# Issuing the first weight load ahead of the opening barrier in a cached-attention decode kernel

## Chip, cores and metric

One core of one Trainium2 chip. The metric is the device time of one execution in microseconds. A ratio between two kernels is the mean time of one kernel's fast runs over that of the other's in the same rounds, so it is not quite the ratio of the medians that are quoted beside it. Some of the traces' records are of single packets of the 16 DMA engines; where a number comes from those and not from a printed view, the text says so. These records name no engine: packets are put down to one engine because each of them starts within some 0.01 us of another's end.

## The reference

A decode step of two sequences with one token each: layernorm, attention with 32 heads over a cache of 8192 positions, an output projection, and a gated feed-forward block. The caches are what matters: 2 x 2 x 32 x 8192 x 128 bf16 values, 268 MB, each read once.

```python
def _A_ref(x, k_cache, v_cache, wq, wo):            # x: (2, 1, 512)
    q = (x @ wq).reshape(B, Sq, Hq, Dh)...           # wq: 512 x 4096
    scores = jnp.einsum("bhqd,bhkd->bhqk", q, k) * (Dh ** -0.5)
    p = _softmax(scores, axis=-1)
    o = jnp.einsum("bhqk,bhkd->bhqd", p, v)
    return o... @ wo                                 # wo: 4096 x 512
h = x + _A_ref(_layernorm(x), A_k_cache, A_v_cache, A_wq, A_wo)
h2 = h + _B_ref(_layernorm(h), B_W_gate, B_W_up, B_W_down)
```

## The kernel before

SyncE does all the large loads. Two SBUF buffers, K and V, each hold one tile of 8.39 MB (128 rows of 64 KB). wq is put into the upper half of V before V's first own tile, so the first V load has to wait for the projection that reads wq. Each engine's program begins with a drain and a barrier that the framework emits (four small constants on POOL, then all five engines meet); what the kernel writes comes behind it.

```python
nc.scalar.dma_start(x_row, A_x[:, 0]).then_inc(sem_x, 16)
nc.sync.dma_start(V[:, SLOT:], A_wq.rearrange("(p c) n -> p (c n)", c=DC)).then_inc(sem_wq, 16)
nc.sync.dma_start(
    wo_rows, A_wo[128 * DR:].rearrange("(p r) n -> p (r n)", r=4)).then_inc(sem_wl, 16)
load(K, A_k_cache, 0, k_sem[0])
# ... constants on POOL, layernorm of x on VectorE (cut) ...
pe.wait((sem_wq, 16), t_xlT, t_zero)      # projection: 32 matmuls over wq
# ... (cut)
sp.wait(t_q)
load(V, A_v_cache, 0, v_sem)              # V's first tile overwrites wq
# ... in each of the 15 later turns (cut):
sp.wait((d2s, 2 * o - 1), tokp("kf", p))  # K free again
load(K, A_k_cache, o, k_sem[0])
sp.wait(tokp("pv", p))                    # V free again
load(V, A_v_cache, o, v_sem)
```

The softmax here doesn't subtract the row's maximum and nothing guards it: scores larger than these inputs give would overflow.

Of the kernel before, what the change touches and what calls it, by code (L numbers as in the profile page):

```python
# [39 lines left out]
def bass_sequential_preLN__gqa_block_cached__glu_gated_reglu__decode_kernel(  # L40
# [16 lines left out]
    DC = D // 128  # L57
# [5 lines left out]
    SLOT = J * Dh  # L63
# [16 lines left out]
    with ExitStack() as es:  # L80
        def S(name):
            return es.enter_context(nc.semaphore(name))

        def sb(name, shape, dt):
            return es.enter_context(nc.sbuf_tensor(name, shape, dt))
# [14 lines left out]
        sem_x, sem_wq, sem_wl, sem_out = S("x"), S("wq"), S("wl"), S("out")  # L100
# [6 lines left out]
        V = sb("V", [128, 2 * SLOT], BF16)  # L107
# [62 lines left out]
        def kv_rows(cache, o):  # L170
            hq, b = divmod(o, B)
            return cache[b, A * hq:A * hq + A].rearrange("h (p j) d -> (h p) (j d)", p=128 // A)
# [4 lines left out]
        if True:  # L177

            def program():

                def load(x, cache, o, sem, k0=0, k1=2 * J):
                    nc.sync.dma_start(
                        x[:, k0 * Dh:k1 * Dh], kv_rows(cache, o)[:, k0 * Dh:k1 * Dh]).then_inc(sem, 16)

                nc.scalar.dma_start(x_row, A_x[:, 0]).then_inc(sem_x, 16)
                nc.sync.dma_start(V[:, SLOT:], A_wq.rearrange("(p c) n -> p (c n)", c=DC)).then_inc(sem_wq, 16)
                nc.sync.dma_start(
                    wo_rows, A_wo[128 * DR:].rearrange("(p r) n -> p (r n)", r=4)).then_inc(sem_wl, 16)
                load(K, A_k_cache, 0, k_sem[0])
# [57 lines left out]
                for k, row in enumerate((x_row, lnx_row)):  # L247
                    rv = row.rearrange("b (n c) -> b c n", c=DC)
                    for c in range(DC):
                        i = nc.tensor.transpose(  # L250
                            Tp[0][:].bitcast(BF16)[:, (k * DC + c) * B:(k * DC + c + 1) * B], rv[:, c, :], ident[0:B, 0:B])
# [9 lines left out]
                for i in range(2):  # L261
                    for c in range(DC):
                        for t in range(4):
                            n = (2 * t + i) * 512
# [20 lines left out]
                for r in range(2):  # L285
                    for h in range(2):
                        i = nc.tensor.matmul(
                            Sp[r][64 * h:64 * h + 64, 0:A * NQ], lhsT=ident[:].rearrange("p (n r) -> p r n", r=2)[:, r, :],
                            rhs=qT[:], start=True, stop=True)
# [184 lines left out]
                for r in range(DR):  # L474
                    i = nc.tensor.matmul(
                        Op[1][32 * (r % 4):32 * (r % 4) + B, :], lhsT=O_all[:, r, :], rhs=X[:, r * D:(r + 1) * D],
                        start=(r < 4), stop=(r >= DR - 4))
# [249 lines left out]
                for h in range(A):  # L727
                    for c in range(DC):
                        i = nc.tensor.matmul(
                            Wp[:, c * B:(c + 1) * B], lhsT=wv[:, h, c, :], rhs=O_keep[:, h, :],  # L730
                            start=False, stop=True, skip_group_check=True)
# [7 lines left out]
                for c in range(DC):  # L739
                    i = nc.tensor.matmul(Sp[0][:, 0:B], lhsT=onesn[:], rhs=hb[:, c * B:(c + 1) * B],  # L740
                                         start=(c == 0), stop=(c == DC - 1))
# [47 lines left out]
                for k in range(2):  # L789
                    i = nc.tensor.matmul(Sp[0][:, 32:32 + B], lhsT=onesn[:], rhs=vh[:, k * B:(k + 1) * B],  # L790
                                         start=(k == 0), stop=(k == 1))
# [20 lines left out]
                for n, (f, k) in enumerate(order):  # L812
                    pe.wait((sem_wd[k], 16))
                    kp = 128 if f < 10 else FR
                    for m in range(4):
                        i = nc.tensor.matmul(  # L816
                            Op[0][32 * m:32 * m + B, 0:128], lhsT=hd[0:kp, f * B:(f + 1) * B],
                            rhs=(wdn[:, f, :] if f < 10 else wd_last[:])[:, 128 * m:128 * m + 128],
                            start=False, stop=(n == FC - 1), skip_group_check=True)
# [12 lines left out]
                nc.sync.wait_ge(sem_out, 16 * B)  # L832

            program()

    return nc
# [28 lines left out]
```

## Time and profile before

| | before |
|---|---|
| time, median of the first 3 runs | 657.58 us (657.36 to 657.63) |
| span of the profiled execution | 656.1 us |
| read from HBM | 281.05 MB, 428 GB/s over the span |
| busiest engine (VectorE) | 66% |
| SyncE's queue, share of the 16 DMA engines | 99.3% |

The lines themselves stand in the prediction. In the chain and timeline views the first number is a start in us from the beginning of the span and the second a duration; for a DMA piece of the chain these are its issue and the time to its landing.

### The profile page before, as it was taken

What the parts mean: (1) busy time and instruction counts of PE and PEld (TensorE: products, weight loads), DVE (VectorE), ACT (ScalarE), POOL (GpSimd) and SP (SyncE); (2) the same over time, 40 slices, a digit from 0 to 9 for tenths busy, and PEclk for the clock granted to TensorE, in tenths of its full rate; (3) what the DMA queues carried; (4) which work ended last, traced back from release to release, by engine and by line L of the source; (5) the groups of instructions that cost most, each with busy time, mean ns of one, the idle gap of its engine ahead of it and who ended that gap; (6) DMA issues with size and microseconds to landing.
All of it is one profiled execution on the core that took longest, in us unless ns stands there. A gap on an engine that the chain in (4) does not pass through costs nothing.

```text
span 656.1 us, 8543 instructions
## 1 busy us (share of the span) xinstructions
PE 371.9 (57%) x3480; PEld 236.3 (36%) x3481; DVE 432.7 (66%) x275; ACT 304.6 (46%) x719; POOL 88.7 (14%) x96
## 2 busy tenths in 40 slices
PE   2374573756457385545637555474755537464677
PEld 0152441615134161423416242251623325152445
DVE  1187493947849395793939669393875939488771
ACT  1355362735536173443716445371653527254460
POOL 4000020030301103030120303003030300303000
PEclk9856556566655756665575667557565655766657
DMA  9999999999999999999999999999999999999997
GB/s 408 401 439 440 447 435 404 443 443 443 416 428 439 447 439 400 443 443 447 420 420 439 447 435 404 447 439 447 428 412 443 443 435 420 431 439 415 430 423 313
DMA packets 6324, 281.16 MB, mean 429 GB/s; under 512 B 710, under 2 KB 812, under 8 KB 1324
## 3 DMA queue, kind: packets, MB, share of 16 engines
q1 hardware_dynamic: 6308, 281.05, 99.3%
q8 instruction: 5, 0.08, 0.1%
q14 instruction: 3, 0.02, 0.0%
q10 hardware_dynamic: 8, 0.00, 0.0%
HBM read 281.05 MB, written 0.00 MB: 428 GB/s over the span
## 4 chain that ended last, share of the span: by engine, by line
DMA 64%; PE 22%; ACT 7%; DVE 6%; issue 1%; DVEq 0%; SPq 0%
DMA K<-in_A_k_cache_dram 59%; PE T L395 16%; ACT kT L578 7%; DMA K<-in_B_W_gate_dram 5%; PE S L378 5%; DVE prod L552 2%; DVE prod L561 2%; DVE X L561 1%; DVE X L552 1%; DVE scores L566 0%; PE O L816 0%; PE O L764 0%; DVEq L617 0%; DVEq L598 0%; DVE kT L824 0%
## 5 line engine op out<-in xcount | busy, mean ns | idle before, releaser
L578 ACT ACTIVATE kT<-T 128x1024 bf16<-128x1024 bf16 x160 | 160.0, 1022 | 196.5 <-PE T L395 192.7
L395 PE MATMUL T<-ident_f,K 128*128 128x128 f32 x640 | 161.7, 416 | 100.7 <-DVEq L598 94.8
L552 DVE TENSOR_TENSOR X<-K,q_c 128x11264 bf16<-128x11264 bf16 x15 | 90.4, 6026 | 172.5 <-DMA K<-in_A_k_cache_dram 172.5
L418 PE MATMUL O<-V,e 128*16 128x512 bf16 x1024 | 117.2, 596 | 111.1 <-ACT e L506 77.0
L395 PEld LDWEIGHTS T<-ident_f,K 128*128 128x128 f32 x640 | 114.5, 213 | 102.8 <-DVEq L598 96.8
L561 DVE TENSOR_TENSOR prod<-prod 128x5632 bf16<-128x5632 bf16 (+1 forms) x68 | 104.3, 1533 | 4.0
L552 DVE TENSOR_TENSOR prod<-K,q_c 128x11264 bf16<-128x11264 bf16 x17 | 102.3, 6020 | 6.2 <-DMA K<-in_A_k_cache_dram 4.5
L506 ACT ACTIVATE e<-scores 32x88 bf16<-32x88 f32 x128 | 51.1, 399 | 105.4 <-DVEq L609 103.9
L418 PEld LDWEIGHTS O<-V,e 128*16 128x16 bf16 x1024 | 30.3, 116 | 184.9 <-ACT e L506 101.8
L561 DVE TENSOR_TENSOR X<-X 128x5632 bf16<-128x5632 bf16 (+3 forms) x60 | 92.0, 1533 | 3.7
L378 PE MATMUL S<-q_c,kT 128*128 128x8 bf16 x1280 | 60.8, 171 | 40.1 <-ACT kT L578 40.0
L378 PEld LDWEIGHTS S<-q_c,kT 128*128 128x128 bf16 x1280 | 51.5, 107 | 75.6 <-ACT kT L578 73.7
L533 POOL MEMSET O_l<- 128x32 bf16 x13 | 1.7, 130 | 427.6 <-DVEq L615 427.6
L538 POOL COPY rsel<-rows 128x112 bf16<-128x112 bf16 x14 | 40.4, 2885 | 39.5 <-DVEq L615 38.7
L431 PE MATMUL Ob<-sel,os_sb 128*128 128x4 f32 x136 | 29.3, 339 | 11.0 <-ACT os_sb L581 11.0
L506 ACT ACTIVATE e<-S 32x40 bf16<-32x40 f32 x128 | 31.9, 249 | 2.4 <-PE S L378 0.9
L431 PEld LDWEIGHTS Ob<-sel,os_sb 128*128 128x128 f32 x136 | 27.8, 303 | 12.9 <-ACT os_sb L581 12.8
L506 ACT ACTIVATION_READ_ACCUMULATOR e<-scores 32x1 f32 x128 | 28.1, 219 | 0.0
L506 ACT ACTIVATION_READ_ACCUMULATOR e<-S 32x1 f32 x128 | 25.6, 200 | 1.5
L540 POOL TENSOR_TENSOR O_l<-O_cur,mask 128x32 bf16<-128x32 bf16 x14 | 23.1, 1652 | 0.0
L549 POOL COPY q_c<-q_all 128x144 bf16<-128x144 bf16 x16 | 15.2, 950 | 45.5 <-PE O L418 33.1
L578 ACT ACT_TABLE_LOAD x15 | 19.2, 1283 | 0.3
(106 smaller groups left out, 136.2 us busy)
## 6 DMA issues: line engine op xcount, KB each, us to landing
K<-in_A_k_cache_dram SPq DMA_DIRECT2D x2, 4096.0 KB, 21.8
V<-in_A_wq_dram SPq DMA_DIRECT2D x1, 4096.0 KB, 12.5
V<-in_A_v_cache_dram SPq DMA_DIRECT2D x1, 4096.0 KB, 24.9
X<-in_A_wo_dram SPq DMA_DIRECT2D x1, 3584.0 KB, 18.0
V<-in_A_v_cache_dram SPq DMA_DIRECT2D x1, 3072.0 KB, 32.1
K<-in_B_W_up_dram SPq DMA_DIRECT2D x1, 1376.0 KB, 30.1
K<-in_B_W_gate_dram SPq DMA_DIRECT2D x1, 1376.0 KB, 33.1
V<-in_A_v_cache_dram SPq DMA_DIRECT2D x1, 1024.0 KB, 33.9
```

What stands on the lines that cost most here:

```text
L378: i = nc.tensor.matmul(Sp[p % 2][:, A * jj:A * jj + 2 * A], lhsT=kv_[:, k, r, :], rhs=q_c[:, 2 * A * r:2 * A * r + 2 * A], start=(r == 0), ...
L395: i = nc.tensor.transpose(Tp[g % 2][:, k * 128:(k + 1) * 128], k_t[:, j:j + 2, :].rearrange("p j d -> p (j d)").bitcast(F32), ident_f[:])
L418: i = nc.tensor.matmul(Op[0][c:c + 16, :], lhsT=e_t[q][:, j // VJ, :], rhs=v_t[:, j:j + VJ, :].rearrange("p j d -> p (j d)"), start=(q == ...
L431: i = nc.tensor.matmul(Ob[:, 0:A], lhsT=os_sb[:, jj * Dh:(jj + 1) * Dh], rhs=sel[:, A * jj:A * jj + A], start=(jj == 0), stop=(jj == VJ - 1))
L506: i = nc.scalar.activation(out=e_t[q][h, j0 // VJ:j1 // VJ, :].rearrange("p g (j a) -> p g j a", a=A)[:, :, :, a], in_=src(h, a), func=ACT ...
L533: pool.run(e.memset(o_window(o - 1)[0], 0.0))
L538: e.tensor_copy(out=rsel[:, :, o % B, :], in_=bass.AP(x.tensor, x.offset, [list(x.ap[0]), [DR - OS, A], [1, DR]]))
L540: e.tensor_tensor(out=w, in0=O_cur[:].unsqueeze(2).broadcast_to([128, A, NM]), in1=mask[:, off // 4:off // 4 + OS // 4 * (A - 1) + 1:OS // ...
L549: nc.gpsimd.tensor_copy(out=q_c[:], in_=q_all[:, o]).then_inc(g2d, 1)
L552: return nc.vector.tensor_tensor(out=pr[:, 0:JC, :], in0=tile(K, p)[:, 0:JC, :], in1=q_c[:, Q2:QW].unsqueeze(1).broadcast_to([128, JC, Dh] ...
L561: run(nc.vector.tensor_tensor(out=pr[:, 0:JC, 0:w], in0=pr[:, 0:JC, 0:w], in1=pr[:, 0:JC, w:2 * w], op=ALU.add))
L578: to_pe(nc.scalar.activation(out=kT[gg % 2][:], in_=Tp[gg % 2][:].bitcast(BF16), func=ACT.Copy))
```

## The change

The intent is to let the DMA engines begin during the barrier rather than after it. wq's load has nothing to wait for: its target is untouched SBUF and its source is an input. The helper takes the instruction just emitted out of the block and puts it in front of SyncE's first drain.

```diff
+                def ahead_of_barrier(emit, engine):
+                    block = nc.cur_bb.bb.instructions
+                    n = len(block)
+                    emit()
+                    new = block[n:]
+                    del block[n:]
+                    at = next(i for i, x in enumerate(block)
+                              if isinstance(x, mybir.InstDrain) and x.engine == engine)
+                    block[at:at] = new
+
+                ahead_of_barrier(lambda: nc.sync.dma_start(
+                    V[:, SLOT:], A_wq.rearrange("(p c) n -> p (c n)", c=DC)).then_inc(sem_wq, 16), nc.sync.engine)
                 nc.scalar.dma_start(x_row, A_x[:, 0]).then_inc(sem_x, 16)
-                nc.sync.dma_start(V[:, SLOT:], A_wq.rearrange("(p c) n -> p (c n)", c=DC)).then_inc(sem_wq, 16)
```

## The prediction

> **What bounds the kernel now.** I read the page from the top: the engine shares, the slices, the queues. Then the chain of waits, to see what a loop turn waits for; then SyncE's instructions in order of time, to see how far ahead each load is issued; last the first microseconds, since that is all that the diff touches.
>
> ```profile
> span 656.1 us, 8543 instructions
> PE 371.9 (57%) x3480; PEld 236.3 (36%) x3481; DVE 432.7 (66%) x275; ACT 304.6 (46%) x719; POOL 88.7 (14%) x96
> DMA  9999999999999999999999999999999999999997
> q1 hardware_dynamic: 6308, 281.05, 99.3%
> HBM read 281.05 MB, written 0.00 MB: 428 GB/s over the span
> ```
>
> No engine is over 66%. The DMA row is 9 in every slice but the last, and SyncE's queue q1 alone fills 99.3% of the 16 DMA engines. The kernel is a stream of 281 MB.
>
> A busy queue could still be one that waits now and then, so I look at the pace of a turn. In the chain of waits, in order of time:
>
> ```profile
> 1.72 33.28 DMA K<-in_A_k_cache_dram
> 48.57 25.14 DMA K<-in_A_k_cache_dram
> 87.26 25.15 DMA K<-in_A_k_cache_dram
> 125.96 25.15 DMA K<-in_A_k_cache_dram
> 617.24 33.08 DMA K<-in_B_W_gate_dram
> ```
>
> The first column is the issue, the second the time to landing. A K load lands at 73.71, 112.41, 151.11: one turn is 38.70 us. A turn moves one K and one V tile of 8.39 MB (128 partitions x 64 KB), so 16.78 MB / 38.70 us = 433.5 GB/s, or 19.35 us for a tile. The K load issued at 48.57 needs 19.35 us of pure transfer and lands at 73.71, so its first bytes move at about 54.36: it stood 5.8 us behind the V load before it. SyncE in order of time has the V loads 18.5 us after the K loads; with their median 26.0 us to landing, a V load stands 26.0 - 19.35 = 6.65 us in line. The queue never runs dry: both waits for a free buffer end some 6 us before the transfer is due. The chain names PE and ScalarE between the K pieces (22% and 7%), but that work releases a buffer that the queue does not need yet. In the tail the W_gate load takes 33.08 us from issue to landing for 1.4 MB: it too stands in line. It lands at 650.32, and what follows to 656.1 is short work on data already there or right behind it.
>
> So the end is: the moment at which the queue starts moving, plus a transfer of fixed length, plus a tail of 5.8 us. The start in time order, and the instructions around the opening barrier:
>
> ```profile
> 0.81 0.40 SPq L186 DMA_DIRECT2D V<-in_A_wq_dram  x1
> 0.81 0.55 ACTq L185 DMA_DIRECT2D kT<-in_A_x_dram  x1
> 1.26 0.41 SPq L187 DMA_DIRECT2D prod<-in_A_wo_dram  x1
> 1.72 0.42 SPq L182 DMA_DIRECT2D K<-in_A_k_cache_dram  x1
> 13.37 3.58 PE L265 MATMUL O<-V,xlT 128*2 128x512 bf16 x32 [7.94 <-DMA V<-in_A_wq_dram]
> ```
>
> ```profile
> L850 SPq DRAIN  x1: 7/7/7, 0.0 to 0.0; - x1
> L850 POOLq DRAIN  x1: 186/186/186, 0.4 to 0.4; - x1
> L850 SPq EVENT_SEMAPHORE  x1: 17/17/17, 0.7 to 0.7; - x1
> ```
>
> ```profile
> 1.60:1.80 0.20, 0.00 (x0) 0.00 (x0) 0.20 (x1) 0.20 (x1) 0.20 (x2) 1.00 0.04 10
> 1.80:2.00 0.20, 0.00 (x0) 0.00 (x0) 0.10 (x1) 0.20 (x1) 0.14 (x2) 1.00 5.60 1475
> ```
>
> SyncE reaches its drain at 0.0, the very start of the span, passes the barrier at 0.7 and issues wq at 0.81; the large packets start at about 1.82, by the trace's records of single packets (the windows table shows none before 1.80; a packet counts where it starts, hence the 1475 GB/s). All DMA engines idle for these 1.8 us. POOL, with four memsets and a 186 ns drain at 0.4, is what the barrier waits for longest.
>
> **What the Trainium skill says.** "Perfetto Trace Analysis", section "Summary: the profiler window per engine type": for a load issued by SyncE the profile's interval covers descriptor generation and the push, not the movement of the data. The trace agrees: 0.40 us of issue for a load that lands 12.5 us after it began. "DMA: Bandwidth & Descriptors", section "Specifications", gives about 0.6 us to the first byte for this path; here 1.82 - 1.21 = 0.61 us after the issue ended. The same table has a fabric ceiling of 435 GB/s, and 433.5 is 99.7% of it; it also has an HBM limit of about 358 GB/s for a core, which this trace exceeds, so the measurement decides. The same page, section "Queues, rings and completion order", says that a DMA engine with work on several queues takes turns by packet; that matters for x below. No page says whether a drain behind a load's issue waits for the load's data. That is the one fact of the change which the trace of before can't show either, for there no load stands ahead of a drain.
>
> **The change part by part.** Nothing is removed or added: the order of instructions differs on SyncE alone, whose first load stands ahead of its drain instead of behind the barrier. Every other engine has the same list.
>
> Moved, wq: the issue goes from 0.81 to where the drain stood, 0.00. It takes the same 0.40 us, and the first packets should come 0.61 us later, at about 1.01 instead of 1.82. Gain at the head of the queue: 0.81 us. If the issue costs a few hundredths more at this place, 0.75.
>
> Moved, the drain: it comes at 0.40 instead of 0.00, and SyncE reports to the barrier at about 0.41. POOL's drain ends at about 0.4 + 0.19 = 0.59, so the barrier should open at 0.7 as now, with some 0.15 us to spare. Were it 0.2 us late, the other engines would start that much later, and they have slack: PE waits 7.94 us for wq before L265.
>
> Moved, wo and K: they become first and second behind the barrier, so 1.26 goes to 0.81 and 1.72 to 1.26. Worth nothing by itself: they stand behind 4.19 MB of wq, which take 4.19 MB / 433.5 GB/s = 9.7 us.
>
> Unmoved, x: ScalarE still issues it at 0.81, but wq's packets now hold the engines by then. A wq packet is a row of 32 KB, 1.2 us at 27 GB/s per engine (433.5 / 16). If x's 2 KB waits for one or two of these, VectorE's first use moves from 2.94 to about 5 (an estimate), and the layernorm and transposes, which take 2.7 us (2.94 to 5.63), end near 8. wq lands at 13.3 - 0.8 = 12.5. Hidden. Even behind all of wq, the projection would come some 3 us later than now and the first V load be issued at 20 instead of 17.00, with K in transfer until 34. Hidden still.
>
> The stream: wq, wo, K at 0.81 us earlier; the first V is issued by the projection's end, 17.00, which follows wq and goes to about 16.2, with 18 us of queue before it. Each later issue is released by engine work that begins at a landing, so all move with the landings. Nothing in the 38.70 us turn depends on where it began. Tail: 5.8 us behind W_gate's landing, unchanged.
>
> Sum: -0.81 at the head, 0 in the turns, 0 in the tail: -0.8 us. 657.58 - 0.8 = 656.8 us, a change of 0.12%.
>
> **The rivals.** First: the drain waits for the load's data. Then the barrier opens at about 12.5, wo is issued and 1.0 us (0.40 + 0.61) of empty queue follows, with the handshake perhaps 1.5 us, and the x chain starts at 12.5, so that the projection ends near 12.5 + (5.63 - 0.81) + 3.7 = 21 us, still ahead of the time at which V is needed. Net -0.8 + 1.5 = +0.7: 658.3 us. Against it: a drain of 7 ns on a sequencer empties an instruction pipeline, and a load's issue is over when its descriptors are pushed. I give it 5%.
>
> Second: the gain is hidden, because something else than the head of the queue sets the pace: the time stays at 657.6. For it: the chain shows PE and ScalarE work in each turn. Against it: 5.8 and 6.65 us in line before each transfer. It is also what would be seen if the load, issued at 0.0, found its queue not ready before 0.8. 10%.
>
> Third: more than 0.81. The 16 engines begin wq spread over a good 1 us now (by the packet records, their first packets start from 1.82 to 2.89), and a load is complete when the last of them is. In the changed kernel wq is issued alone, not beside x; were that spread less, another 0.3 us could come. Speaks against it: nothing shows that x causes the spread. 656.4. 15%.
>
> Fourth: wq's packets collide with instruction fetches at the start of an engine. The instruction queues moved only 0.08 MB and 0.02 MB in all, and an engine that starts 1 or 2 us late is still ahead of wq. No effect on the time.
>
> **Range and chances.** The three runs before lie within 0.27 us (657.36 to 657.63), so a median of the same kind is good to about 0.15. With the rivals on either side I put the range for 8 in 10 at 656.3 to 657.3. Two per cent would be 13 us, which no rival reaches: a load 1.8 us into a span can gain at most these 1.8 us, and even the drain that waits costs about a tenth of the threshold. Faster 0.5%, within 2% 99%, slower 0.5%.
>
> **What the profile of the changed kernel would show.** The wq issue as SyncE's first row at about 0.0; large packets at about 1.0 instead of 1.82; SyncE's semaphore row still at 0.7; wo at about 0.81 and K at 1.26; L265's first matmul at about 12.6 instead of 13.37; x's first use later than 2.94 but before 9; the chain's first K landing at 34.2 instead of 35.00 and the turns still 38.70 apart; W_gate's landing near 649.5, the span 655.3. Wrong if SyncE passes the barrier at 12 (the drain waits), if the packets still start at 1.8 with the issue at 0.0 (the queue isn't ready), or if the landing times move by less in later turns than in the first (the stream isn't the bound).

## The result

The changed kernel took 656.92 us in the median of 6 runs (656.52 to 657.05), before 657.51 us in 6 runs (657.36 to 657.63); the ratio is 0.999, with a 95% interval of 0.9977 to 1.0003. Within 2%, 0.6 us less by the medians, where 0.8 was predicted. This interval includes 1, so the set alone leaves the difference unproven, though the times of the two kernels do not overlap; the repeat below has an interval that leaves it out. The profiled execution took 656.90 us against 657.45.

The page of the changed kernel, span, slices and queue:

```profile
span 655.6 us, 8544 instructions
DMA  9999999999999999999999999999999999999997
q1 hardware_dynamic: 6308, 281.05, 99.4%
```

Nothing of the picture has changed: the same bytes through the same full queue. The start of the changed kernel, first in order of time, then the instructions at the barrier, then the windows (their last two columns are the DMA engines' share and GB/s, a packet counted where it starts):

```profile
0.00 0.40 SPq L195 DMA_DIRECT2D V<-in_A_wq_dram  x1
0.80 0.34 SPq L198 DMA_DIRECT2D prod<-in_A_wo_dram  x1
0.80 0.55 ACTq L197 DMA_DIRECT2D kT<-in_A_x_dram  x1
1.19 0.46 SPq L182 DMA_DIRECT2D K<-in_A_k_cache_dram  x1
...
7.01 0.68 DVE L242 BATCH_NORM_STATS2 bst<-kT 2x6 f32<-2x512 bf16 x1 [3.98 <-DMA kT<-in_A_x_dram]
...
12.26 3.58 PE L276 MATMUL O<-V,xlT 128*2 128x512 bf16 x32 [2.56 <-DMA V<-in_A_wq_dram]
```

```profile
L861 SPq DRAIN  x1: 121/121/121, 0.5 to 0.5; - x1
L861 SPq EVENT_SEMAPHORE  x1: 17/17/17, 0.7 to 0.7; - x1
```

```profile
0.00:1.20 1.20, 0.00 (x0) 0.00 (x0) 0.00 (x0) 0.00 (x0) 0.41 (x5) 1.00 0.96 273
```

The issue is at 0.00, and packets begin before 1.2; by the packet records the first at 1.02, where it was 1.82. SyncE's drain, 7 ns before, takes 121 ns behind a load and does not wait for the 4 MB: SyncE passes the barrier at 0.7 as before. x's data now moves behind three rows of wq and is complete one row later, and VectorE's first use of it goes from 2.94 to 7.01. It is still hidden: PE waits for wq, not for x.

The chain of waits of the changed kernel, the K loads:

```profile
1.19 33.17 DMA K<-in_A_k_cache_dram
47.34 25.73 DMA K<-in_A_k_cache_dram
86.62 25.20 DMA K<-in_A_k_cache_dram
551.14 25.16 DMA K<-in_A_k_cache_dram
```

The last of these in before:

```profile
551.68 25.15 DMA K<-in_A_k_cache_dram
```

The first landing is 34.36 (1.19 + 33.17) against 35.00: 0.64 us earlier, not 0.81. The second is 73.07 against 73.71, still 0.64; the last of the loop is 576.30, and 551.68 + 25.15 = 576.83 in before: 0.53. The span is 0.5 less. So the gain that reaches the end of this execution is the gain at the first landing, less 0.1 us in the first turns (38.75, 38.74 and 38.72 us where the later ones are 38.70; why they are longer is not known). Most of what was missing was missing at once, by 34 us.

The packet records show how. An engine serves 8 of the 128 rows of a tile, and the landing follows the end of the latest engine's eighth row by 0.44 us in both kernels (34.56 and 35.00; 33.92 and 34.36). At the end of wo the engines stand spread over 13.48 to 14.24 us in before and 12.49 to 13.11 in the changed kernel. The median engine is 0.97 us earlier (13.66 and 12.69). From there to the end of the first K tile an engine needs 19.32 us, but one engine also serves a 16 KB instruction fetch: that packet takes 1.03 us and the 64 KB packet after it 2.90 instead of 2.42, together 1.50 us. That engine is the last one, in both kernels. In before it was hit from a place near the middle (13.74 to 13.84; the records leave three candidates), in the changed kernel it was the very latest engine, at 13.11. Its gain is 0.63 to 0.73 us, and the load's is 0.64.

### The profile page after: what moved, and what is told of

Read it like the earlier page. It is cut to its first block, busy times and chain, and to the rows that moved or that the text cites. A ratio compares the mean times of both kernels' runs of the same rounds, so it can differ in the third digit from the quotient of the medians.

```text
span 655.6 us, 8544 instructions
## 1 busy us (share of the span) xinstructions
PE 373.4 (57%) x3481; PEld 238.7 (36%) x3481; DVE 432.9 (66%) x275; ACT 304.7 (46%) x719; POOL 88.9 (14%) x96
## 4 chain that ended last, share of the span: by engine, by line
DMA 64%; PE 24%; ACT 7%; DVE 4%; issue 1%; SPq 0%; DVEq 0%; ACTq 0%
DMA K<-in_A_k_cache_dram 59%; PE T L406 17%; ACT kT L589 7%; DMA V<-in_A_v_cache_dram 5%; PE S L389 5%; DVE prod L572 1%; DVE X L572 1%; PE O L429 1%; DVE X L563 1%; DVE prod L563 1%; DVE scores L577 0%; PE S L775 0%; PE O L775 0%; PE O L827 0%; ACT e L517 0%
## 5 line engine op out<-in xcount | busy, mean ns | idle before, releaser
L406 PE MATMUL T<-ident_f,K 128*128 128x128 f32 x640 | 165.8, 424 | 100.4 <-DVEq L609 95.0
L406 PEld LDWEIGHTS T<-ident_f,K 128*128 128x128 f32 x640 | 117.9, 217 | 102.6 <-DVEq L609 97.1
L442 PE MATMUL Ob<-sel,os_sb 128*128 128x4 f32 x136 | 27.7, 327 | 11.0 <-ACT os_sb L592 11.0
L442 PEld LDWEIGHTS Ob<-sel,os_sb 128*128 128x128 f32 x136 | 26.2, 287 | 13.3 <-ACT os_sb L592 13.2
## 6 DMA issues: line engine op xcount, KB each, us to landing
K<-in_B_W_gate_dram SPq DMA_DIRECT2D x1, 1376.0 KB, 32.5
```

What stands on the lines that cost most here:

```text
L406: i = nc.tensor.transpose(Tp[g % 2][:, k * 128:(k + 1) * 128], k_t[:, j:j + 2, :].rearrange("p j d -> p (j d)").bitcast(F32), ident_f[:])
L442: i = nc.tensor.matmul(Ob[:, 0:A], lhsT=os_sb[:, jj * Dh:(jj + 1) * Dh], rhs=sel[:, A * jj:A * jj + A], start=(jj == 0), stop=(jj == VJ - 1))
```

## The experiments

Theory A: the end is the moment at which the queue starts plus a fixed transfer, slope one; in its refined form, for each engine by itself, and the latest engine sets every landing. Against it: the gain is hidden (B), it is wq's earlier landing and not the queue's head that counts (C), the barrier's delay costs (D), and others named below. All runs were correct. They were made in two sets of four, each with its own 9 runs of before: the change once more, wo in place of wq, all three ahead and the loads held back (before: 657.44 us in the median); then wo again, x alone, x with wq and the four rows (657.42).

### The change once more

No edit.

> The changed kernel once more, for a closer interval and a second look at its spread. Theory A (the head of the DMA queue sets the end, and each microsecond there is one at the end): 0.6 to 0.8 us under before, near 656.9 us. Theory A with its refinement (a load is complete when the last of 16 DMA engines is, and an engine that has to fetch instructions between two packets is later by about 1.5 us, so what is gained at the end is what THAT engine gained at the start): the first K landing is earlier than before's by what the latest engine gained, and the end by the same to 0.2 us; the gain can therefore differ from execution to execution by the 1 us over which the engines' starts are spread. Rival B (hidden): 657.5 us.

656.65 us (656.38 to 656.66), ratio 0.9986, interval 0.9972 to 0.9999, which leaves out 1. Its first K landing is 1.19 + 33.09 = 34.28, 0.72 us before that of before; its profiled execution took 656.66, 0.79 less. Over both sets the changed kernel's 11 runs have a mean of 656.71, all 24 runs of before one of 657.50: 0.79 us. That is the predicted 0.8 as a mean; single executions lie 0.45 to 1.1 us below 657.50.

### wo's small load ahead in place of wq

```diff
-  ahead_of_barrier(wq load);  nc.sync wo load;  load(K)
+  ahead_of_barrier(wo load);  nc.sync wq load;  load(K)
```

> The 0.5 MB load of the last rows of wo stands ahead of the barrier in place of wq; wq is first behind the barrier, issued at 0.81 us as in before. Theory A (what counts is when the queue begins to move): the same gain as the change, 0.6 to 0.8 us, near 656.9 us, if the 1.2 us that 0.5 MB takes cover the time until wq's packets are there (issued at 0.81, first packets at 1.8; wo's packets would end at about 2.2). Rival C (what counts is when wq and with it the query projection is done): no gain, 657.5 us, for wq then lands no earlier than in before (13.3 us).

> The kernel with the small wo load ahead of the barrier again, because its five times fell in two groups (656.5 and 656.7; 658.0 to 658.3) and its one profile was of the fast group. Theory A with its refinement: the time of the profiled execution minus before's equals the shift of the latest engine's mark at the second K load (about 72.4 us in the fast profile, 73.26 in before), to 0.1 us, whichever group the profile is from; the slow group is then executions in which one engine was later at the start or was hit by two instruction fetches (about 1.5 us more each), and is random. Rival E (wo first costs something systematic, such as a hole in the queue before wq): a hole of about 1.4 us after wo's packets in every slow execution, on all engines alike.

Two submissions of the same kernel: 656.49, 656.72, 657.98, 658.07 and 658.28 us (ratio 1.0004, 0.9991 to 1.0018), then 657.66, 657.23, 656.57, 656.29 and 658.27 us (0.9994, 0.998 to 1.0007). It is spread over 2 us where the others are within 1. The projection's first matmul in the profile of the first submission (656.49 us) and of the second (657.66 us):

```profile
13.72 3.52 PE L275 MATMUL O<-V,xlT 128*2 128x512 bf16 x32 [7.77 <-DMA V<-in_A_wq_dram]
```

```profile
14.58 3.58 PE L275 MATMUL O<-V,xlT 128*2 128x512 bf16 x32 [8.61 <-DMA V<-in_A_wq_dram]
```

In the first, wq lands later than in before (before: 13.37), and yet the execution is 0.96 us shorter: rival C falls, it is not wq's landing that counts. In the second, the windows of the start show packets that begin late. The same half microsecond, first then second (one 32 KB packet begins in it, and five):

```profile
3.00:3.50 0.50, 0.00 (x0) 0.00 (x0) 0.07 (x2) 0.00 (x0) 0.50 (x2) 1.00 0.17 66
```

```profile
3.00:3.50 0.50, 0.00 (x0) 0.00 (x0) 0.02 (x1) 0.00 (x0) 0.50 (x2) 1.00 0.99 328
```

By the packet records four of the 16 engines there begin wq only at 3.39 to 3.66, when their share of wo is over by 3.1, and their first rows of wq take 1.9 to 2.2 us instead of 1.21. When wq is done, four engines are 1.0 us behind the median. So wo's 0.5 MB cover the time until wq's packets come only just, and in this execution not on all engines; the other slow ones were not profiled. Neither form of my expectation was quite right: the delay isn't on all engines (rival E), and it is not the random lag of one engine either. Why wq's packets reach four engines late, 2.6 to 2.9 us after the issue began, is open.

### All three loads ahead

```diff
-  wo load and load(K) behind the barrier
+  ahead_of_barrier(wo load); ahead_of_barrier(load(K))
```

> All three loads that SyncE issues at the start (wq, wo, K) stand ahead of the barrier. Three issues of 0.4 us make SyncE reach the barrier at about 1.35 us instead of 0.5, so all other engines start 0.6 to 0.7 us later. Theory A: the same as the changed kernel to 0.2 us (656.9), as wo and K stand in line behind wq anyway and the other engines have slack before wq lands. Rival D (the late barrier costs): slower than the changed kernel by the 0.6 to 0.7 us, near before's 657.5.

656.72 us (656.5 to 656.83), ratio 0.9988 (0.9975 to 1.0002): as the changed kernel. Its barrier:

```profile
L861 SPq DRAIN  x1: 125/125/125, 1.4 to 1.4; - x1
L861 SPq EVENT_SEMAPHORE  x1: 17/17/17, 1.7 to 1.7; - x1
```

The barrier opens at 1.7 instead of 0.7, later than I expected, and costs nothing: rival D falls. The first microsecond of the four other engines is slack.

### The loads held back

```diff
+  sp.wait(t_const)      # POOL's constants are done
   wq load; wo load; load(K)
```

> The kernel before with the three first loads of SyncE held back until POOL has made its constants, about 5.85 us instead of 0.81: the head of the queue is moved the other way, and six times as far. Theory A: slope one, +5.0 us (662.5 us), every landing 5.0 us later to the end. Rival B (slack of some 6 us in each turn absorbs it, or part of it): between 657.5 and 660 us.

662.73 us (662.36 to 662.83), ratio 1.0078 (1.0064 to 1.0092). In order of time, and in the chain of waits:

```profile
5.86 0.40 SPq L212 DMA_DIRECT2D V<-in_A_wq_dram  x1
...
18.27 3.58 PE L266 MATMUL O<-V,xlT 128*2 128x512 bf16 x32 [12.84 <-DMA V<-in_A_wq_dram]
```

```profile
6.78 33.45 DMA K<-in_A_k_cache_dram
556.89 25.16 DMA K<-in_A_k_cache_dram
```

The issue moved by 5.05 us, the first packets by 5.07, the first K landing by 5.23 (40.23 against 35.00), the loop's last by 5.22 (582.05 against 576.83) and the median time by 5.29. Rival B, by which the slack of some 6 us in each turn absorbs part of it, falls: that slack belongs to the buffers, not to the queue. This is the clearest of the runs, being far outside the spread.

### x alone, and x with wq

```diff
-  nc.scalar.dma_start(x_row, A_x[:, 0]).then_inc(sem_x, 16)
+  ahead_of_barrier(that load, nc.scalar.engine)   # wq behind the barrier, or ahead of it too
```

> Only ScalarE's 2 KB load of x stands ahead of the barrier, wq stays behind it as in before. Theory A: wq's packets start at 1.8 as in before, so no gain: 657.4 us, within 0.3. Rival F (part of the gain comes from wq not being issued beside x, which spreads the engines' starts by 1 us): wq's first packets are spread by 0.3 to 0.4 us instead of 1.07, and up to 0.3 us is gained.

> Both wq on SyncE and x on ScalarE stand ahead of the barrier. Theory A: the same as the changed kernel (656.6 to 656.9): wq's packets start at 1.0; x lands near 2.2 instead of 7.0 and the layernorm ends 4 to 5 us earlier, which was hidden anyway. If x's delay to 7.0 had cost something, this kernel is the faster one.

x alone: 657.88 us (657.7 to 658.11), ratio 1.0006 (0.9992 to 1.002), slower by some 0.4 us. In order of time:

```profile
0.13 0.55 ACTq L196 DMA_DIRECT2D kT<-in_A_x_dram  x1
1.10 0.40 SPq L195 DMA_DIRECT2D V<-in_A_wq_dram  x1
```

I had overlooked that ScalarE's issue takes 0.55 us and its drain comes after it: the barrier opens at 1.0 and wq's issue is 0.29 us later than in before. By the slope of one that is the loss, to 0.1 to 0.2 us. The starts of the engines spread over 0.95 us by the packet records (2.12 to 3.07), where rival F, x as the cause of the spread, asked for 0.3 to 0.4 instead of before's 1.07. F has no support. (The spread is a matter of the execution too: 0.83 in the changed kernel, 0.47 in the next one.)

x with wq: 656.65 us (656.6 to 656.92), ratio 0.9988 (0.9975 to 1.0002), the changed kernel's time. VectorE takes x at 4.75 instead of 7.01, and that is worth nothing. I had x landing near 2.2; by the packet records its data moved at 2.90 and 3.16 and was complete at 4.42, for wq, issued 0.12 us before it, was already on the engines.

### A few more microseconds for one engine

```diff
+  for i in range(4):
+      nc.sync.dma_start(V[i:i + 1, 0:SLOT], kv_rows(A_k_cache, 0)[i:i + 1, 0:SLOT]).then_inc(sem_j, 16)
   wo load; load(K)
-  sp.wait(t_q)
+  sp.wait(t_q, (sem_j, 64))
   load(V, A_v_cache, 0, v_sem)
```

> The changed kernel with four idle loads of one 32 KB row each behind wq, which by their shape should all go through a single one of the 16 DMA engines: 128 KB more, 4.8 us of that one engine at 27 GB/s. Refined theory A (the last engine sets the end): slower than the changed kernel by 4.8 us less what that engine was ahead of the latest, so by 3 to 4.8 us (659.8 to 661.6 us), and that one engine is the last at every later landing. Rival G (the mean rate over all engines sets the end): 128 KB / 433.5 GB/s = 0.3 us, so 657.0 us.

661.07 us (660.58 to 661.48), ratio 1.0054 (1.004 to 1.0067), so 4.4 us above the changed kernel's 656.65 of the first set, for 0.05% more bytes. The issues and the K loads of its chain:

```profile
0.80 1.16 SPq L200 DMA_DIRECT2D V<-in_A_k_cache_dram  x4
```

```profile
2.40 34.92 DMA K<-in_A_k_cache_dram
50.08 26.80 DMA K<-in_A_k_cache_dram
```

By the packet records the four rows are done one after another at intervals of 1.21 us, one engine ending wo at 17.55 when the others end it by 13.31. It is the last at the first K tile (36.87, the next engine 33.64), and at the three loads after that the latest engine is 2 to 4 us behind the next. Rival G, the mean rate, said 0.3 us and is out by more than a factor of ten: the latest engine counts. The delay reaches the others through the landing: the second K load is issued at 50.08 instead of 47.34, and by the packet records the 16 engines are then busy for 96% of the time from 50 to 60 us, where they are busy for 99.6% in the changed kernel.

### All profiled executions together

The latest engine's mark is the moment at which the last of the 16 engines ends its share of the second K tile, by the packet records; by then both early instruction fetches are over. Each number is the difference to before, whose mark is 73.26 us and whose profiled execution took 657.45 us.

| kernel | first packet | mark | time |
|---|---|---|---|
| the change | -0.79 | -0.63 | -0.55 |
| the change once more | -0.79 | -0.73 | -0.79 |
| wo in place of wq | -0.79 | -0.91 | -0.96 |
| the same, again | -0.78 | +0.33 | +0.21 |
| three ahead | -0.79 | -0.76 | -0.80 |
| held back | +5.07 | +5.22 | +5.30 |
| x alone | +0.30 | +0.51 | +0.30 |
| x with wq | -0.78 | -0.82 | -0.80 |
| four rows on one engine | -0.79 | +3.28 | +3.62 |

The mark at 73 us gives the time at 657 us within 0.1 us in six cases, within 0.34 in all nine. The first packet alone is within 0.25 us in seven, and for x alone it is the better of the two; it fails for the slow execution of wo and for the four rows, in which some engines were late. None of the kernels beats the changed one by more than its spread.

## Why the prediction was right

- The bound: right. The queue is full from the first packet to the tail, and holding back the loads shows a slope of one (5.05 us put in, 5.29 us at the end).
- The head of the queue, 0.81 us: right on average (0.79 us over 11 runs) and in place (issue at 0.00, first packet at 1.02). The prediction treated the 16 engines as one. In the profiled execution the term was worth 0.64 at the first landing, because the engine that sets it gained less than the median one; the first turns took another 0.1. The third rival had seen that the latest engine matters, but looked for the cause in x, and x isn't it. That one execution's gain comes near 0.8 is in part chance: it depends on which engine the fetch falls to.
- Instruction fetches: wrong. The fourth rival set them aside for their few bytes, with no effect on the time. One of 16 KB cost the engine that serves it 1.50 us, and that engine was the last one in both kernels. As before has this cost too, only the difference between the two places counts, some 0.2 us.
- The drain: right that it doesn't wait and that the barrier opens at 0.7; the drain takes 121 ns, not 7. The first rival (658.3 us) is out.
- wo, K: issued at 0.80 and 1.19, for 0.81 and 1.26 predicted, worth nothing, as the kernel with all three ahead confirms.
- x: hidden, as said, but mis-sized. It waited for three rows and then one more for its completion, and was used at 7.01, not near 5; the estimate had allowed for one or two rows in all. PE's wait for wq shrank from 7.94 to 2.56 us.
- The projection began at 12.26, not 12.6: the latest engine of wq was 1.13 us earlier (11.86 against 12.99), and no instruction fetch falls into that load.
- The tail moved with the rest. The chain's last long wait is now for V's last piece and not for W_gate, which changed nothing at the end. W_gate itself landed at 617.18 + 32.5 = 649.7, predicted 649.5.
- One test that I had set was too strict: landings moved by 0.64 early and 0.53 late, which I had said would mean that the stream isn't the bound. The run with the loads held back shows that it is.

## What to carry to other kernels

Where the DMA queue is never empty, as here, the time at which it first gets a load was paid in full at the end, and an opening barrier is time that the first load can use if it depends on nothing; measure it by moving the load the other way, where the effect is larger than the spread. Do not put a minor load ahead of the barrier while the important one stays behind it: the barrier then opens later, as x alone showed. And count 16 DMA engines, not one: a load ends with the latest of them, so a few rows on a single engine cost nearly what that engine takes (4.4 us of 4.8 here), not their share of the bandwidth.

## What the Trainium skill lacked or had wrong

- No page says whether a drain behind a load's issue waits for the load's data. Here it took 121 ns (125 behind three issues, 137 on ScalarE) against 7 or 8 without one, and did not wait for the data.
- "Runtime: NRT & Kernel Launch", section "Instruction fetch mechanics", calls the cost of crossing a 16 KB boundary mostly hidden. For the sequencer that may be; the DMA engine that serves the fetch lost 1.50 us in its stream (1.03 for the packet, 0.48 more for the row after it), and in before and in the changed kernel it was the last engine at the first K landing and at the second.
- "DMA: Bandwidth & Descriptors", section "Specifications", has an HBM limit of about 358 GB/s for a core without a condition; a turn of the loop moved 433.5 GB/s on one core. The page's own section "Bandwidth" says that this figure is for both cores of a pair streaming, so it is the table's row that misleads. Its 0.6 us to the first byte agrees: 0.61 us in before and 0.62 after the change.
- The same page, section "Queues, rings and completion order", has an engine drain a packet of typically 9 to 17 descriptors before it turns to another queue. With x behind wq's eight rows for each engine, x's data went at 5.27 us, after three rows, and its completion one row later, at 6.52: the engine turned to x's queue in the middle of wq's rows. Why after three is open.
- No page says that the first rows after an idle time are slower: in the changed kernel each engine's first row of wq took 1.3 to 2.1 us, most later ones 1.21.
